# A fused attention and mixture-of-experts kernel: a list turned three units later, first weights loaded in four separate steps, one more side step in a slot

## The chip, the cores and the metric

The kernel runs on one core of one Trainium2 chip. The metric is the device time in microseconds (us) of one execution; lower is better. The core's engines are TensorE (PE, with its weight loads shown as PEld), VectorE (DVE), ScalarE (ACT), GpSimd (POOL) and SyncE (SP). In this kernel SP issues nearly all direct transfers, and POOL issues the indirect ones (gathers and scatters through a list of rows).

## The reference

Eight batches of attention with 12 heads, 448 tokens and head size 64, with a sigmoid in place of the softmax, followed by a mixture of experts over all 3584 tokens (768 wide, 8 experts, 1024 hidden units). All data is float32.

```python
scores = scale * np.matmul(q, k.transpose(0, 1, 3, 2)) - np.log(S)
attn = 1.0 / (1.0 + np.exp(-scores))
x = np.matmul(attn, v)            # then (batch*seq, heads*head_dim) = (3584, 768)

logits = x @ w_gate
e_idx = np.argmax(logits, axis=1)
gate_w = softmax(logits)[np.arange(N), e_idx]
eom = 1.0 / (1.0 + np.exp(-(x @ w_output_gate)))
for e in range(E):
    mask = e_idx == e
    h = np.maximum(x[mask] @ w1[e], 0.0)
    out[mask] = gate_w[mask, None] * eom[mask, e, None] * (h @ w2[e])
```

## The kernel before, in words

**Attention.** `attention` runs 168 units, one after the other. The text counts them backwards from the end of attention, as the code does (`self.unit(u - U * NG)`): unit -168 is the first, unit -1 the last. Seven units make a group, which holds two pairs of heads. In unit u, PE computes scores of u (L632), ACT applies the sigmoid (L634), and PE multiplies the result of unit u-2 with the values (L641). The scores have two places in PSUM, so the scores of u+2 need the sigmoid of u to be done. Where a pair of heads is complete, DVE adds its two halves out of PSUM and turns the sum (`evict`: L644 or L648, L654, L655). After every second group, PE multiplies four such results with the gate weights (`gates`, L671); these read the tiles that L654 writes. One such place is unit -11.

**Work beside attention.** `unit(u)` is called at the head of each unit and puts extra work into the engines' queues at that place: the first tokens are sorted to experts before attention ends. At unit -28 the first expert's layer-1 weights start to load (`load_w`, L416, issued by SP), and from unit -22 on they are split into a high and a low part (L426 on ACT, L427 on DVE). At unit -18 the first list of tokens is turned (`spread_lists`: a DVE transpose at L388, then twelve small POOL copies at L392 to L395), POOL gathers the rows of the first slot (L404), and SP loads two more lists from DRAM (`load_list`, L383). At unit -13 these two are turned by a second `spread_lists`; at unit -10 the whole layer-2 weights of the first expert are loaded in four pieces of 768 KB (`load_w2`); at unit -8 the gathered rows are turned (`turn_x`, L452).

**Slots.** Then come slots of 256 tokens of one expert each. Slot 0, 1 and 2 are made from the first six batches. `slot` runs layer 1 for eight blocks of hidden units f (`layer1_mm`, L467 and L468; ACT copies one PSUM half at L475, DVE adds the other at L476 into `gl`), and the PSUM places of layer 1 are three, so block f+3 waits for L476 of block f. Then come four outputs of layer 2 (L490 to L492; ACT scales them at L502, POOL scatters them at L504 after the second and the fourth). Beside it the next slot's rows are gathered, turned (L452) and split (L427), and its weights are split (`split_w1`: ACT L430, DVE L433; `split_w2`: ACT L426, DVE L427). An order "high, low" in layer 1 means that PE needs the low part of weight pair k (L433) at steps d = 2k and 2k+1 of block 0.

**Side work.** The generator `side` in `build` holds the rest of the routing: the last batch's gates, the table of all remaining slots (`table(True)`, DVE lines L299 to L368 in five pieces, each on one partition), and the loading and turning of the remaining lists. `slot` takes one step of it (`next(side, None)`) after each of the blocks f = 0 to 6, once more in slot 0, and after the second, third and fourth layer-2 output.

**Order.** Nothing reorders the instructions: `manual_schedule` keeps each engine's queue in the order in which the code emits it. An engine that waits holds up all that stands behind it in its queue.

Of the kernel before, what the change touches and what calls it, by code (L numbers as in the profile page):

```python
# [51 lines left out]
class Kernel:  # L52
# [455 lines left out]
    def slot(self, cur, nxt, side=None, begun=False, drain=False):  # L508
        nx = self.load_slot(*nxt) if nxt is not None else None
        if drain:  # L510
            self.gather(dict(lx=self.lxb[:, 1], xg=self.half_x(1)))
            self.nc.gpsimd.drain()
        self.split_w2(0)
        for f in range(8):
            self.layer1(f, begun and f == 0)
            if f:
                self.high_low(f - 1)
            if f in (1, 3, 5):
                self.split_w2(f // 2 + 1)
            if side is not None and f < 7:  # L520
                next(side, None)
        self.high_low(7)
        if side is not None and begun:
            next(side, None)
        self.load_w2(nx)
        if nx is not None:
            self.high_w1(0)
            self.turn_x(nx)
            for k in range(3):
                self.split_x(nx, k)  # L530
            self.low_w1(0)
        for i, (t, n) in enumerate(((0, 0), (0, 1), (1, 0), (1, 1))):
            self.layer2(cur, t, n, self.ys[t])
            if i < 2 and nx is not None:
                self.split_w1(i + 1)
            if side is not None and i > 0:
                next(side, None)
        return nx

# [177 lines left out]
    def unit(self, u):  # L717
        if u == -161:
            self.row_words()
        if u == -154:  # L720
            self.init_list()
        if u == -31:
            self.tgen = self.table(False)
        if -31 <= u < -28:
            next(self.tgen)
        if u == -28:
            self.s0 = self.slot_regs(self.tab_e, 0, self.lts[:, 0], self.lxs[:, 0])
        s = self.s0 if u >= -28 else None
        for d in range(6):
            if u == -28 + d:  # L730
                self.load_w(s, self.w1, self.w1r, [d], 1)
            if u == -22 + 2 * d:
                self.split_w1_row(d)
        if u == -21:
            self.load_list(self.tab_e, 0, self.lr_e[0][0:8], 8)
        if u == -18:
            self.spread_lists(self.lr_e[0], self.lts[:, 0:1], self.lxs[:, 0:1])
            self.gather(s, ROWS_E)
            for k in range(1, EARLY):
                self.load_list(self.tab_e, k, self.lr_e[1][8 * k - 8:8 * k], 8)  # L740
        if u == -13:
            self.spread_lists(self.lr_e[1], self.lts[:, 1:EARLY], self.lxs[:, 1:EARLY])
        if u == -10:
            self.load_w2(s)
        if u == -8:
            self.turn_x(s)
        for k, at in enumerate((-6, -5, -4)):
            if u == at:
                self.split_x(s, k)
# [120 lines left out]
```

## Time and profile before

| | us |
|---|---|
| median of three runs (lowest, highest) | 802.03 (799.63, 804.19) |
| the profiled execution's own time | 802.2 |
| its span, first to last instruction | 800.4 |
| PE busy in the span | 784.6 (98%) |
| DVE busy | 498.4 (62%) |
| ACT busy | 494.9 (62%) |
| POOL busy | 338.4 (42%) |

The durations below come from that one profiled execution, and times of day are microseconds from its span's start. Attention ends and slot 0 begins at about 285; slot 0 ends at about 320, slot 1 at 356, slot 2 at 390. A busy PE is not PE at its peak, so time that PE loses shows in two ways: as idle time, and as work that takes longer than the same work elsewhere. "Granted clock" (PEclk) is the share of TensorE's full clock that the chip gave in a stretch.

### The profile page before, as it was taken

The numbers are of one execution on the slowest core, as the hardware profiler recorded it, in microseconds if no ns is written. First come the engines' busy times: TensorE is split into PE (matmuls) and PEld (weight loads), VectorE is DVE, ScalarE is ACT, GpSimd is POOL, SyncE is SP. The second block draws the span as 40 slices with busy tenths as digits, with TensorE's granted clock in tenths as the row PEclk, the third lists the DMA queues.
The fourth block names the chain that finished last, engine by engine and source line by source line (L and its number), as shares of the span: only waits on it lengthen the run. The fifth ranks groups of instructions, "written<-read, shape, count | busy, mean of one in ns | idle before, by whom it ended". The sixth has DMA issues, their size and how long they took to land. (4 is left out here: it accounts for less than half of the span.)

```text
span 800.4 us, 15091 instructions
## 1 busy us (share of the span) xinstructions
PE 784.6 (98%) x5772; PEld 582.3 (73%) x5772; DVE 498.4 (62%) x731; ACT 494.9 (62%) x665; POOL 338.4 (42%) x454
## 2 busy tenths in 40 slices
PE   9999999999999899899999999999999999999996
PEld 4333433333333379799999999999999999999885
DVE  2344435444455667877785657766667767667687
ACT  5666666666668556556665556655666557565685
POOL 4003302310333456647646265543646725445344
PEclk9999999999999999999999999999999999999999
DMA  6353553525448420237228471182274211749382
GB/s 255 131 209 128 158 200 139 193 85 208 170 173 347 154 90 21 77 123 266 75 75 290 166 270 51 49 312 79 61 259 156 64 45 41 267 131 336 110 314 59
DMA packets 32311, 126.80 MB, mean 158 GB/s; under 512 B 5536, under 2 KB 7824, under 8 KB 28257
## 3 DMA queue, kind: packets, MB, share of 16 engines
q1 hardware_dynamic: 22288, 100.81, 35.5%
q0 software_dynamic: 9936, 24.88, 9.4%
q8 instruction: 50, 0.82, 0.4%
q14 instruction: 37, 0.29, 0.1%
HBM read 153.15 MB, written 23.64 MB: 221 GB/s over the span
## 5 line engine op out<-in xcount | busy, mean ns | idle before, releaser
L467 PE MATMUL ps<-rounded 128*128 128x512 f32 x672 | 234.8, 393 | 2.0 <-DVE gl L476 2.0
L634 ACT ACTIVATE a<-ps,bias_s 128x896 f32<-128x896 f32 x168 | 169.2, 1008 | 102.5 <-PE ps L632 96.1
L468 PE MATMUL ps<-rounded 128*128 128x256 f32 x672 | 188.1, 280 | 0.0
L404 POOL DMA_INDIRECT plain<-x_dram,lxs x120 | 170.2, 1418 | 38.3 <-issue 37.0
L490 PE MATMUL ps<-w2h,h 128*128 128x384 f32 x480 | 160.6, 335 | 0.0
L492 PE MATMUL ps<-w2h,h 128*128 128x384 f32 x480 | 160.4, 334 | 0.0
L491 PE MATMUL ps<-w2l,h 128*128 128x384 f32 x480 | 160.4, 334 | 0.0
L632 PE MATMUL ps<-kqv 64*64 64x448 f32 x1344 | 158.6, 543 | 0.5 <-ACT a L634 0.4
L641 PE MATMUL ps<-a,kqv 64*64 64x448 f32 x1344 | 156.7, 538 | 0.0
L427 DVE TENSOR_TENSOR w2l<-plain,w2h 128x1536 fp32r<-128x1536 f32 x60 | 105.3, 1758 | 78.3 <-ACT w2h L426 68.1
L467 PEld LDWEIGHTS ps<-rounded 128*128 128x128 f32 x672 | 125.7, 187 | 31.3 <-DVE gl L476 2.7
L504 POOL DMA_INDIRECT out<-y,lts x28 | 59.7, 2132 | 172.3 <-ACT y L502 92.5
L468 PEld LDWEIGHTS ps<-rounded 128*128 128x128 f32 x672 | 127.0, 189 | 0.0
L641 PEld LDWEIGHTS ps<-a,kqv 64*64 64x64 f32 x1344 | 51.7, 134 | 75.5 <-issue 74.8
L632 PEld LDWEIGHTS ps<-kqv 64*64 64x64 f32 x1344 | 48.8, 133 | 75.1 <-issue 62.3
L433 DVE TENSOR_TENSOR rounded<-plain,rounded 128x2048 fp32r<-128x2048 f32 x46 | 102.8, 2284 | 0.0
L426 ACT CAST w2h<-plain 128x1536 fp32r<-128x1536 f32 x60 | 88.2, 1473 | 5.4 <-PE ps L671 4.4
L490 PEld LDWEIGHTS ps<-w2h,h 128*128 128x128 f32 x480 | 90.1, 188 | 0.7
L491 PEld LDWEIGHTS ps<-w2l,h 128*128 128x128 f32 x480 | 90.1, 188 | 0.1
L492 PEld LDWEIGHTS ps<-w2h,h 128*128 128x128 f32 x480 | 90.1, 188 | 0.0
L475 ACT COPY gl<-ps 128x256 f32<-128x256 f32 x112 | 41.7, 372 | 77.7 <-PE ps L468 73.3
L430 ACT CAST rounded<-plain 128x2048 fp32r<-128x2048 f32 x46 | 87.6, 1904 | 0.0
(186 smaller groups left out, 649.0 us busy)
## 6 DMA issues: line engine op xcount, KB each, us to landing
plain<-w SPq DMA_DIRECT2D x68, 768.0 KB
plain<-w SPq DMA_DIRECT2D x48, 1024.0 KB
kqv<-kqv SPq DMA_DIRECT2D x23, 1344.0 KB
x_dram<-xt SPq DMA_DIRECT2D x8, 1344.0 KB
plain<-w SPq DMA_DIRECT2D x6, 512.0 KB
plain<-x_dram,lxs POOLq DMA_INDIRECT x120
kqv<-kqv SPq DMA_DIRECT2D x1, 896.0 KB
lst<-plain POOLq DMA_DIRECT2D x1, 726.0 KB
```

The lines of the kernel that those rows point to most:

```text
L404: self.nc.gpsimd.indirect_dma_start(out=s["xg"][:, g], out_offset=None, in_=x4, in_offset=bass.IndirectOffsetOnAxis(ap=s["lx"][:, g:g + 1] ...
L426: self.nc.scalar.copy(hi, raw)
L427: self.nc.vector.tensor_tensor(lo, raw, r32(hi), ALU.subtract)
L433: self.nc.vector.tensor_tensor(self.w1p[1][k], self.w1r[:, 2 * k:2 * k + 2], r32(self.w1p[0][k]), ALU.subtract)
L467: nc.tensor.matmul(ps, wh[d][:, c], self.xc[:, d].rearrange("p a t -> p (a t)"), start=(d == 0), stop=False)
L468: nc.tensor.matmul(ps[:, 0:TS], wl[d][:, c], self.xc[:, d, 0], start=False, stop=(d == 5))
L490: nc.tensor.matmul(ps, hh[:, f, tk], wh, start=(f == 0), stop=False)
L491: nc.tensor.matmul(ps, hh[:, f, tk], wl, start=False, stop=False)
L492: nc.tensor.matmul(ps, hl[:, f, tk], wh, start=False, stop=(f == 7))
L632: nc.tensor.matmul(ps[half[h], j, 0:S], kg[half[j], e, 0, o:o + 64], kg[half[j], e, 1], start=True, stop=True)
L634: nc.scalar.activation(at[u % 4], ps[:, :, 0:S], AF.Sigmoid, bias=self.bias_s, scale=1.0 / math.sqrt(D))
L641: nc.tensor.matmul(self.ps_o[e][h][half[j], 0:S], v[half[h], 6 if i == 3 else 3 * e + c, j], a[half[h], j], start=(i in ((0, 3 if h else 4 ...
```

## The change

Three edits. In `unit`, the second `spread_lists` (two lists at once) moves from unit -13 to unit -10. The load of the layer-2 weights, four pieces at unit -10, becomes four loads of one piece each at units -9, -7, -5 and -3, each behind a DVE memset of one element of the place that it writes, so that SP's load waits for DVE to get there. In `slot`, a step of the side work is taken behind the first layer-2 output too, so each slot with side work takes one step more, and every later step comes earlier by one, then by two, and so on.

```diff
@@ -533,7 +533,7 @@
             self.layer2(cur, t, n, self.ys[t])
             if i < 2 and nx is not None:
                 self.split_w1(i + 1)
-            if side is not None and i > 0:
+            if side is not None:
                 next(side, None)
         return nx
 
@@ -738,10 +738,12 @@
             self.gather(s, ROWS_E)
             for k in range(1, EARLY):
                 self.load_list(self.tab_e, k, self.lr_e[1][8 * k - 8:8 * k], 8)
-        if u == -13:
+        if u == -10:
             self.spread_lists(self.lr_e[1], self.lts[:, 1:EARLY], self.lxs[:, 1:EARLY])
-        if u == -10:
-            self.load_w2(s)
+        for k in range(4):
+            if u == -9 + 2 * k:
+                self.nc.vector.memset(self.w2r[0:1, 2 * k, 0:1], 0.0)
+                self.load_w(s, self.w2, self.w2r, [2 * k])
         if u == -8:
             self.turn_x(s)
```

In DVE's queue near the end of attention, the turn of the two lists (L388) stood at unit -13, ahead of the eviction (L648, L654) whose tile the gates of unit -11 read (`lt_99` is the turned list, `xh` and `x_161` the evicted sums):

```order
 L655 STREAM_TRANSPOSE xt_164<-x_160 128x14x32
 L427 TENSOR_TENSOR rounded<-plain,rounded 128x1024
-L388 STREAM_TRANSPOSE lt_99<-plain 32x192
 L648 COPY xh<-ps 128x448
 L654 TENSOR_TENSOR x_161<-xh,ps 128x448
```

Now that eviction follows L427 directly. A few rows on, behind the two copies of the gates' results (L683, L678), the turn comes back, and the first of the memsets (L745, into `plain`, where the layer-2 weights land) one unit behind it:

```order
 L683 TENSOR_TENSOR gl_113<-gl_113,ps 64x448
 L678 COPY gl_114<-ps 64x448
-L644 COPY xh<-ps 128x448
+L388 STREAM_TRANSPOSE lt_99<-plain 32x192
+L644 COPY xh<-ps 128x448
+L745 MEMSET plain 1x1
 L654 TENSOR_TENSOR x_158<-xh,ps 128x448
 L655 STREAM_TRANSPOSE xt_164<-x_158 128x14x32
```

In DVE's queue at the border of slot 0 and slot 1, the pieces of the table (L299 to L356) move forward past the split of the third weight pair (the last L433) and past the split (L427) and the sum (L476) with which slot 1 begins:

```order
 L427 TENSOR_TENSOR rounded<-plain,rounded 128x2x256 x3
-L433 TENSOR_TENSOR rounded<-plain,rounded 128x2048 x3
+L433 TENSOR_TENSOR rounded<-plain,rounded 128x2048 x2
 L299 COPY hb<-last_e 1x1
```

```order
 L353 TENSOR_SCALAR hb<-slots,hb 1x15
 L356 SCALAR_TENSOR_TENSOR hb<-hb 1x15 x3
-L476 TENSOR_TENSOR gl_113<-gl_113,ps 128x256
-L481 SCALAR_TENSOR_TENSOR h_2445<-gl_113,h_2444 128x256
-L427 TENSOR_TENSOR w2l_2447<-plain,w2h 128x1536
+L427 TENSOR_TENSOR w2l_2451<-plain,w2h 128x1536
+L476 TENSOR_TENSOR gl_113<-gl_113,ps 128x256
 L358 TENSOR_SCALAR hb<-hb 1x15
```

So the first piece of the table now stands ahead of the third L433, and the fourth ahead of slot 1's first L427 and L476 (the numbers behind `w2l` and `h` differ only in counting). The later steps move too: in POOL's queue the twelve copies of one more list stand ahead of slot 1's first scatter, and those of the next list ahead of slot 2's gather instead of behind it.

## Rows read from the trace of the kernel before

**Rows 1.** The page: busy time of each engine with its share of the span.

```profile
PE 784.6 (98%) x5772; PEld 582.3 (73%) x5772; DVE 498.4 (62%) x731; ACT 494.9 (62%) x665; POOL 338.4 (42%) x454
```

**Rows 2.** The waits of PE over the whole span, longest in total first: who waited for whom, us in total, times, longest.

```profile
PE ps L671 <- DVE x L654: 2.1, 1, 2.1
PE ps L467 <- DVE gl L476: 2.0, 2, 1.5
```

**Rows 3.** DVE in order of time, units -14 to -11: start, duration, what, and in brackets the idle time before it and what ended it.

```profile
255.51 1.24 DVE L427 TENSOR_TENSOR rounded<-plain,rounded 128x1024 fp32r<-128x1024 f32 x1 [0.57 <-ACT rounded L426]
260.96 0.50 DVE L388 STREAM_TRANSPOSE lt<-plain 32x192 f32<-32x192 f32 x1 [4.21 <-DMA plain<-lst]
...
262.00 0.62 DVE L654 TENSOR_TENSOR x<-xh,ps 128x448 f32<-128x448 f32 x1
```

**Rows 4.** PE in order of time: the scores of units -13 and -11, the gates of unit -11 with a wait ahead of them, the scores of unit -10, and those of unit -1.

```profile
255.49 0.93 PE L632 MATMUL ps<-kqv 64*64 64x448 f32 x8
...
258.81 0.98 PE L632 MATMUL ps<-kqv 64*64 64x448 f32 x8
...
262.68 0.95 PE L671 MATMUL ps<-x,wg 128*32 128x448 f32 x6 [2.13 <-DVE x L654]
...
265.64 1.77 PE L632 MATMUL ps<-kqv 64*64 64x448 f32 x8
...
281.67 0.93 PE L632 MATMUL ps<-kqv 64*64 64x448 f32 x8
```

**Rows 5.** ACT in order of time: the sigmoids of units -55 and -43 (six groups earlier, the same places of their groups as units -13 and -1), those of units -13 and -12, and the first split of the layer-2 weights in slot 0.

```profile
187.88 1.01 ACT L634 ACTIVATE a<-ps,bias_s 128x896 f32<-128x896 f32 x1 [0.50 <-PE ps L632]
...
208.16 1.01 ACT L634 ACTIVATE a<-ps,bias_s 128x896 f32<-128x896 f32 x1 [0.49 <-PE ps L632]
...
257.75 1.01 ACT L634 ACTIVATE a<-ps,bias_s 128x896 f32<-128x896 f32 x1 [1.36 <-PE ps L641]
...
264.17 1.01 ACT L634 ACTIVATE a<-ps,bias_s 128x896 f32<-128x896 f32 x1 [4.48 <-remote]
...
288.13 1.48 ACT L426 CAST w2h<-plain 128x1536 fp32r<-128x1536 f32 x1 [4.40 <-PE ps L671]
```

**Rows 6.** Busy time in three stretches: length, then busy us of PE, PEld, DVE, ACT and POOL, the granted clock, the busy share of the DMA engines and GB/s; and, from SP in order of time, the four loads of the layer-2 weights (first issue, time until the last is issued).

```profile
240.00:248.00 8.00, 8.00 (x92) 3.24 (x88) 4.62 (x6) 7.18 (x8) 0.00 (x0) 1.00 1.01 411
252.00:260.00 8.00, 7.86 (x86) 3.08 (x80) 3.64 (x4) 6.18 (x7) 6.54 (x13) 1.00 1.00 362
...
266.00:267.00 1.00, 1.00 (x8) 0.25 (x4) 0.99 (x2) 0.76 (x1) 0.40 (x3) 0.50 1.00 398
...
255.47 8.56 SPq L416 DMA_DIRECT2D plain<-w  x4
```

**Rows 7.** DVE in order of time, end of slot 0 and beginning of slot 1: the three L433 (merged), the first and last row of the table's first piece, slot 1's first L427, the sum of block 0, the first row of the table's fourth piece, the sum of block 1, the first row of the fifth piece, the sum of block 2.

```profile
313.96 6.69 DVE L433 TENSOR_TENSOR rounded<-plain,rounded 128x2048 fp32r<-128x2048 f32 x3
320.57 0.14 DVE L299 COPY hb<-last_e 1x1 f32<-1x1 f32 x1
...
322.77 0.15 DVE L317 SCALAR_TENSOR_TENSOR hb<-hb,ebase 1x8 f32<-1x8 f32 x1
...
326.14 1.74 DVE L427 TENSOR_TENSOR w2l<-plain,w2h 128x1536 fp32r<-128x1536 f32 x1
327.81 0.40 DVE L476 TENSOR_TENSOR gl<-gl,ps 128x256 f32<-128x256 f32 x1
328.14 0.26 DVE L348 TENSOR_TENSOR hb<-hb 1x120 f32<-1x120 f32 x1
...
329.47 0.40 DVE L476 TENSOR_TENSOR gl<-gl,ps 128x256 f32<-128x256 f32 x1
...
331.81 0.15 DVE L358 TENSOR_SCALAR hb<-hb 1x15 f32<-1x15 f32 x1
...
332.86 0.40 DVE L476 TENSOR_TENSOR gl<-gl,ps 128x256 f32<-128x256 f32 x1
```

**Rows 8.** PE in order of time, slot 1: the first matmul of block 0, of block 3 and of block 5.

```profile
320.38 0.39 PE L467 MATMUL ps<-rounded 128*128 128x512 f32 x1
...
328.27 0.50 PE L467 MATMUL ps<-rounded 128*128 128x512 f32 x1 [1.49 <-DVE gl L476]
...
333.31 0.50 PE L467 MATMUL ps<-rounded 128*128 128x512 f32 x1 [0.54 <-DVE gl L476]
```

**Rows 9.** POOL in order of time: the first scatter of slot 1, the first of the twelve copies of a turned list, the second scatter, the first and the last of the eight gathers of slot 2; then DVE's turn of the gathered rows and the three L433 of slot 2 (merged), and PE's first matmul of slot 3 that reads the third weight pair's low part.

```profile
350.11 3.15 POOL L504 DMA_INDIRECT out<-y,lts  x1 [5.76 <-ACT y L502]
...
355.06 0.20 POOL L392 CAST lxs<-wg 32x32 int32<-32x32 f32 x1 [1.80 <-DVE wg L388]
...
359.74 1.41 POOL L504 DMA_INDIRECT out<-y,lts  x1 [2.65 <-ACT gl L475]
361.45 0.99 POOL L404 DMA_INDIRECT plain<-x_dram,lxs  x1 [0.30 <-issue]
...
371.31 0.94 POOL L404 DMA_INDIRECT plain<-x_dram,lxs  x1 [0.30 <-issue]
...
376.84 1.78 DVE L452 STREAM_TRANSPOSE plain<-plain 128x1536 f32<-128x1536 f32 x1 [0.19 <-issue]
...
381.12 6.69 DVE L433 TENSOR_TENSOR rounded<-plain,rounded 128x2048 fp32r<-128x2048 f32 x3
...
391.21 0.28 PE L468 MATMUL ps<-rounded 128*128 128x256 f32 x1
```

## The prediction, made before the changed kernel ran

> **What bounds the kernel now.** I read the page first: PE is busy 98% of the span and no other engine above 62% [rows 1], so time can only come from PE's gaps and from PE work that runs slower than elsewhere. The list of PE's waits is short: 2.1 us once, for DVE's L654, and 2.0 us in two places, for DVE's L476 [rows 2]. The changed lines touch both. Then I read DVE, PE and ACT in order of time around each wait.
>
> The first wait is at unit -11. DVE finished L427 of unit -14 at 256.75 and stood 4.21 us before the turn of the second list (L388), whose data landed only at 260.96. L654, whose tile the gates read, was queued behind it and ended at 262.62 [rows 3]. PE, idle since 260.55, began the gates at 262.68 [rows 4]. That is not all of the price. The reader should compare equal stretches: from unit -13 to unit -1 PE's scores took 281.67 - 255.49 = 26.18 us [rows 4]; the same places of their groups, units -55 to -43, took 208.16 - 187.88 = 20.28 us by ACT's sigmoids, which follow the scores directly there [rows 5]. So 5.9 us are lost in these twelve units, and 2.1 of them are the wait that the list names.
>
> The rest shows in three rows. Behind the wait the granted clock stood at 0.50 [rows 6], the lower of its two levels (1.2 GHz), and the scores of unit -10 took 1.77 us in place of 0.93 [rows 4]. ACT's sigmoid of unit -13 came 1.3 us behind the end of its scores, which held the scores of unit -11 back by 0.3 us (the next-but-one scores need its PSUM place). And ACT's sigmoid of unit -12 began only at 264.17, after 4.48 us of idle that the profile puts down to "remote", while its scores had been done since about 258 [rows 4, 5]; the scores of unit -10, which need its place, started at 265.64, right behind it. So two things held PE back here one after the other: the gates, then ACT. ACT's lateness falls in a stretch in which the DMA engines were fully busy and POOL gathered at the same time; between 240 and 248 they were as busy (1.01, 411 GB/s) without a gather, and PE kept its clock and was never idle [rows 6].
>
> **The list and the weights.** The list's transfer was issued ahead of the layer-2 weights, so its landing at 260.96 is at worst the same. The turn now stands behind L678 of unit -11: without the wait the gates run from about 260.5 to 261.5, the two copies behind them (0.62 each, as L654) end near 262.7, so the turn finds its list there with 1.7 us to spare. What is late next would be ACT: I think that its 4.48 us go too, since the weights, which SP issued from 255.47 to 264.03 beside the gather [rows 6], now begin at unit -9, with the gather nearly over. I keep 0.3 us of loss for the lateness at unit -13, which came when only one piece of the weights had been issued. Gain: 5.9 - 0.3 = 5.6 us. Its bounds are 0 (ACT stays late until 264.17 whatever DVE does) and 5.9.
>
> The four memsets write one element; the nearest row is a copy of one element, 0.14 us [rows 7], so four make 0.6 us of DVE, beside an attention in which DVE has 3.6 to 4.6 of 8 us busy [rows 6]: nothing. SP's loads now wait for DVE: behind each stand only the next piece and the write of the last batch's rows, which waits for the end of attention anyway. The last piece leaves at unit -3, some 4.5 us before the end of attention; a piece of 768 KB takes 2 us at the 398 to 411 GB/s of the full stretches [rows 6]; the first use is ACT's L426 at 288.13, behind attention's end [rows 5], that of the last piece five blocks of layer 1 later. If that cover were gone, ACT and DVE in slot 0 would wait, but it is over 10 us.
>
> **The side step.** In slot 0 the order on DVE decides. From 313.96 to 329.87 DVE has no pause: three L433, the table's first three pieces, L427, L476 of block 0, the fourth piece, L476 of block 1 [rows 7]. PE meets it twice: block 3 waits 1.49 us for L476 of block 0, block 5 0.54 us for that of block 2 [rows 8]. Now the first piece (320.57 to 322.92, 2.35 us) stands ahead of the third L433, which ends at 323.0 in place of 320.65. Block 0 of slot 1 starts at 320.38 and a block takes 2.1 us, so its fifth step needs that low part at 322.0: a new wait of 1.0 us. The fourth piece (328.14 to 329.47, 1.33 us) stands ahead of L476 of block 0, which ends at 329.54 in place of 328.21: block 3 starts at 329.6 in place of 328.27. The new wait lies inside that: it only splits it. Two blocks later block 5 could start at 333.8; L476 of block 2 has the same DVE work ahead of it as before and is done at 333.3, so the wait of 0.54 goes. Against 333.31 PE is 0.5 us later. Cost: 0.5 us. The bounds: 0 if block 0 loses nothing, 1.33 if the wait at block 5 stays.
>
> In slots 1 and 2 POOL's order changes. The twelve copies of one list (0.20 each, 2.4 us in all) stand ahead of slot 1's first scatter, and those of the next ahead of slot 2's gather [rows 9]. The first twelve began at 355.06 behind DVE's turn; that turn now stands one L433 (2.2 us) earlier, so they take from 352.8 to 355.2, and the scatter that began at 350.11 begins then. With 1.4 us for itself and the 6.5 us that the second scatter began behind its end before (359.74 - 353.26), then 1.7 us for the second and 2.4 for the copies, the gather starts at 367.2 in place of 361.45, 5.8 us later; with less lag between the scatters it is 2 us. The gather ends its issue at 372.25 and L452 follows at 376.84 without waiting for it; with an estimated 2 us to land there are 2.6 us to spare, and the third L433 of that slot ends at 387.81, 3.4 us before PE needs it at 391.21 [rows 9]. So 6 us of lateness are covered, and I cost it at 0, with 2 us as the upper end.
>
> By the Trainium skill, page "SBUF — State Buffer", section "SBUF: two separate sides", POOL can't write descriptors while DVE holds the port that they share. The scatter that took 3.15 us beside L433 against 1.41 us without one agrees [rows 9]; by that rule a gather that slides further into slot 2 meets more of DVE's long rows, which is the third rival below.
>
> **The sum.** 802.2 (the profiled execution) - 5.6 + 0.5 = 797.1. The three runs shown have their median 0.2 lower, so I say 797.0.
>
> **Rivals.** First, the list wasn't the last to come. If ACT's signal is late for a reason that the change doesn't touch, the scores of unit -10 still wait for 265.2, PE idles and loses its clock as before, and only the 0.5 of the side step is left: 802.5. For it: ACT's late start ended behind L654, not before, and the profile can't name its cause. Against it: nothing like it shows between 240 and 248 at the same DMA load [rows 6].
>
> Second, the longer wait in slot 1 costs the clock. The waits at blocks 0 and 3 are 1.0 and 2.0 us in place of one of 1.49. Behind the gates' 2.1 us and the thin work after it a stretch of some 3.2 us ran at 0.50, which loses 1.6 us: 798.7. Against it: in the 1.49 us of before nothing fell.
>
> Third, slower: slot 2's gather. If it starts 5.8 us late and each of its eight issues takes twice the 1.41 us that the first seven took on average (371.31 - 361.45), as the scatter beside L433 took twice, it ends at 367.2 + 8 x 2.8 = 389.6, and L452 runs at 391.6, 14.8 us later than before. From 3.4 us on every us is PE's: 11.4 us lost, 797.1 + 11.4 = 808.5. The kernel turns slower than before where L452 slips by more than 8.5 us, to 385.4 or later. For it: gather, lists and the next weights fall together there. Against it: DVE's work in layer 1 is the same as before, and the gather ran beside it at 1.41.
>
> **How the numbers follow.** Chances: the forecast 0.61 (own range 795.5 to 799), no gain at unit -11 0.18, the clock lost in slot 1 0.12, the late gather 0.09, of which nearly all ends above 802. What can be told from no change is 0.5%, here 4 us: faster means below 798.0. The forecast lies below it in about four of five cases of its own range (0.49), the clock rival in one of four (0.03): faster 0.52. Slower, above 806, only the gather at its worst and an unlucky mix: 0.07. Same: 0.41. The range from 794.8 to 802.7 takes in the first rival and leaves out the gather and a gain beyond the 5.9.
>
> **What would show it.** Right: no PE wait for L654; L388 at unit -10 without idle time before it; units -13 to -1 in 20.3 to 20.8 us at a granted clock of 1.00; the four loads apart by two units each; a wait of PE at block 0 of slot 1 for L433 and one of about 2 us at block 3, none at block 5. Wrong: ACT's sigmoids still several us behind their scores near unit -12; a granted clock below 1.00 around block 3 of slot 1; PE waits at the beginning of slot 3 for L433, with L452 of slot 2 waiting for its gather. The forecast as a whole fails if the twelve units keep more than 2 us of their loss.

## The result: 0.8% slower, and the profile after

| | median, us | lowest to highest | runs |
|---|---|---|---|
| before | 800.08 | 798.37 to 804.19 | 18 |
| changed | 806.61 | 802.47 to 809.05 | 18 |

The ratio is 1.0076, with a 95% interval of 1.0064 to 1.0089. The forecast was 797.0, the range 794.8 to 802.7: the sign was wrong. The profiled execution of the changed kernel took 806.6 us, its span 804.9.

The page of the changed kernel, busy time of each engine; beside [rows 1] POOL has 4 us more and PE 2 us:

```profile
PE 786.6 (98%) x5772; PEld 584.8 (73%) x5772; DVE 498.6 (62%) x735; ACT 494.0 (61%) x665; POOL 342.6 (43%) x454
```

The waits of PE over the changed kernel's whole span, as in [rows 2] (who waited for whom, us in total, times, longest):

```profile
PE ps L490 <- ACT y L502: 4.8, 2, 4.1
PE ps L468 <- DVE rounded L433: 3.1, 1, 3.1
PE ps L695 <- DVE rounded L691: 1.3, 1, 1.3
PE ps L574 <- DVEq L825: 1.2, 1, 1.2
PE ps L467 <- DVE gl L476: 0.5, 1, 0.5
```

The wait for L654 is gone. Two new ones stand at the top: for L502, which was in no wait of before, and for L433. To see what they cost, cut the span at the first matmul of each slot. From slot 2 on, a slot in which PE never waits takes 33.28 us; slots 0 and 1 are compared with the kernel before:

| kernel | units -13 to -1 | slot 0 starts | slot 0 | slot 1 | slot 2 | slot 3 to the end |
|---|---|---|---|---|---|---|
| before, as profiled first | 26.18 | 284.78 | 35.60 | 35.94 | 33.28 | 410.8 |
| before, a second profile | 23.00 | 281.79 | 35.62 | 36.10 | 33.28 | 410.7 |
| changed | 20.95 | 280.35 | 36.50 | 38.89 | 39.20 | 410.0 |

Against the second profile of before (an experiment, below) the change gains 1.4 us up to slot 0 and 0.75 behind slot 2, and loses 0.9, 2.8 and 5.9 us in the three slots: 7.4 in all, which is 804.9 - 797.5.

**Units.** In order of time, PE's scores of units -13 and -1 in the changed kernel, and DVE's turn of the list, now at unit -10:

```profile
256.29 0.93 PE L632 MATMUL ps<-kqv 64*64 64x448 f32 x8
...
277.24 0.93 PE L632 MATMUL ps<-kqv 64*64 64x448 f32 x8
...
263.22 0.52 DVE L388 STREAM_TRANSPOSE lt<-plain 32x192 f32<-32x192 f32 x1
```

The turn waits for nothing, and the twelve units take 277.24 - 256.29 = 20.95 us.

**Slots 0 and 1.** POOL in order of time, the changed kernel: the four scatters of the last-but-one batch's rows to the lists (L280), and the first gather of slot 0 behind them.

```profile
278.04 0.99 POOL L280 DMA_INDIRECT lst<-meta,posi  x1 [0.67 <-POOL meta L278]
282.53 0.93 POOL L280 DMA_INDIRECT lst<-meta,posi  x1 [3.50 <-DMA lst<-meta,posi]
287.60 0.93 POOL L280 DMA_INDIRECT lst<-meta,posi  x1 [4.14 <-DMA lst<-meta,posi]
289.93 1.82 POOL L280 DMA_INDIRECT lst<-meta,posi  x1 [1.40 <-DMA lst<-meta,posi]
...
292.18 0.99 POOL L404 DMA_INDIRECT plain<-x_dram,lxs  x1 [0.16 <-issue]
```

The same in the second profile of before:

```profile
279.68 0.99 POOL L280 DMA_INDIRECT lst<-meta,posi  x1 [0.67 <-POOL meta L278]
282.06 0.93 POOL L280 DMA_INDIRECT lst<-meta,posi  x1 [1.40 <-DMA lst<-meta,posi]
285.51 0.93 POOL L280 DMA_INDIRECT lst<-meta,posi  x1 [2.51 <-DMA lst<-meta,posi]
289.00 0.93 POOL L280 DMA_INDIRECT lst<-meta,posi  x1 [2.56 <-DMA lst<-meta,posi]
...
290.33 0.99 POOL L404 DMA_INDIRECT plain<-x_dram,lxs  x1 [0.16 <-issue]
```

Each scatter waits until the one before it has landed. Slot 0 starts 1.4 us earlier in the changed kernel, yet its gather starts 1.9 us later: 11.8 us behind the slot's start in place of 8.5. All that POOL does for the routing stands behind that gather, and in DVE's queue L452 stands behind L276, which waits 5.7 us for POOL's L272. At the border of slots 0 and 1, DVE and PE of the changed kernel in order of time (L299 begins the table's first piece):

```profile
308.55 1.78 DVE L452 STREAM_TRANSPOSE plain<-plain 128x1536 f32<-128x1536 f32 x1 [0.20 <-issue]
...
312.83 4.49 DVE L433 TENSOR_TENSOR rounded<-plain,rounded 128x2048 fp32r<-128x2048 f32 x2
317.23 0.13 DVE L299 COPY hb<-last_e 1x1 f32<-1x1 f32 x1
...
319.40 2.29 DVE L433 TENSOR_TENSOR rounded<-plain,rounded 128x2048 fp32r<-128x2048 f32 x1
...
321.75 0.58 PE L468 MATMUL ps<-rounded 128*128 128x256 f32 x1 [3.12 <-DVE rounded L433]
...
328.39 0.50 PE L467 MATMUL ps<-rounded 128*128 128x512 f32 x1 [0.45 <-DVE gl L476]
```

L452 comes 28.2 us behind the start of slot 0, in both profiles of before at 24.9; in the first of them the three L433 began 29.2 us behind the start [rows 7], now they begin at 32.5.

**Slot 2.** The changed kernel in order of time: POOL's first copy of the twelve, one of the later ones, the two scatters of slot 1, a copy of the next twelve, the first and the last gather of slot 2; DVE's turn of the list and the two rows beside which the slow copies ran; then L452 and what follows it on ACT and PE.

```profile
354.75 2.18 POOL L392 CAST lxs<-wg 32x32 int32<-32x32 f32 x1 [9.28 <-DVE wg L388]
...
358.04 1.71 POOL L395 COPY lts<-wg 32x8 f32<-32x8 f32 x1
...
360.43 1.03 POOL L504 DMA_INDIRECT out<-y,lts  x1 [0.16 <-issue]
366.54 2.45 POOL L504 DMA_INDIRECT out<-y,lts  x1 [5.08 <-ACT w2h L426]
...
372.99 1.00 POOL L404 DMA_INDIRECT plain<-x_dram,lxs  x1 [0.15 <-POOL lts L395]
...
382.10 0.94 POOL L404 DMA_INDIRECT plain<-x_dram,lxs  x1 [0.30 <-issue]
...
354.17 0.51 DVE L388 STREAM_TRANSPOSE wg<-hb 32x192 f32<-32x192 f32 x1
354.62 2.24 DVE L433 TENSOR_TENSOR rounded<-plain,rounded 128x2048 fp32r<-128x2048 f32 x1
...
357.92 1.79 DVE L427 TENSOR_TENSOR w2l<-plain,w2h 128x1536 fp32r<-128x1536 f32 x1 [0.60 <-ACT w2h L426]
...
385.10 1.78 DVE L452 STREAM_TRANSPOSE plain<-plain 128x1536 f32<-128x1536 f32 x1 [9.83 <-DMA plain<-x_dram,lxs]
...
386.91 1.66 ACT L426 CAST rounded<-plain 128x512 fp32r<-128x512 f32 x3 [10.30 <-DVE plain L452]
388.47 0.57 ACT L502 ACTIVATE y<-ps,lts 128x384 f32<-128x384 f32 x1
...
389.10 0.44 PE L490 MATMUL ps<-w2h,h 128*128 128x384 f32 x1 [4.08 <-ACT y L502]
```

Read it as a chain. POOL stands 9.28 us before the first copy, for a turn that DVE reaches only behind two L433; in before the first scatter was issued meanwhile, at 350.11 [rows 9]. The second scatter starts 6.1 us behind the first (the profile names ACT's L426 as what ended its wait, which gives it nothing; but the trace has the first scatter landing 5.3 us behind the start of its issue, at 365.7, and the second begins 0.8 us after that). Then twelve more copies, then the gather. On ACT the three splits of the turned rows (L426) stand ahead of L502, which empties the first output's PSUM place: PE waits 4.08 us for it. And the wait takes the clock with it. Windows of the changed kernel behind it (columns as in [rows 6]):

```profile
388.00:390.00 2.00, 0.90 (x4) 0.91 (x5) 2.00 (x4) 2.00 (x4) 0.00 (x0) 0.86 0.00 0
390.00:392.00 2.00, 2.00 (x8) 2.00 (x7) 2.00 (x2) 2.00 (x3) 0.41 (x1) 0.50 0.00 0
392.00:394.00 2.00, 2.00 (x11) 2.00 (x10) 2.00 (x2) 1.58 (x2) 2.00 (x1) 0.79 0.00 0
394.00:396.00 2.00, 2.00 (x14) 1.88 (x13) 2.00 (x1) 0.86 (x2) 0.75 (x1) 1.00 0.37 147
```

PE is busy from 390 on, yet its records count 8 matmuls in 390 to 392 and 14 in 394 to 396, at the full clock: the lower level (1.2 GHz) adds 1.8 us to the wait, 5.9 in all.

### The profile page after: what moved, and what is told of

It is laid out like the page before. It is cut to its first block, busy times and chain, and to the rows that moved or that the text cites. A ratio compares the mean times of both kernels' runs of the same rounds, so it can differ in the third digit from the quotient of the medians.

```text
span 804.9 us, 15094 instructions
## 1 busy us (share of the span) xinstructions
PE 786.6 (98%) x5772; PEld 584.8 (73%) x5772; DVE 498.6 (62%) x735; ACT 494.0 (61%) x665; POOL 342.6 (43%) x454
## 5 line engine op out<-in xcount | busy, mean ns | idle before, releaser
L404 POOL DMA_INDIRECT plain<-x_dram,lxs x120 | 168.6, 1405 | 38.1 <-issue 36.3
L427 DVE TENSOR_TENSOR w2l<-plain,w2h 128x1536 fp32r<-128x1536 f32 x60 | 105.4, 1759 | 66.1 <-ACT w2h L426 66.0
L433 DVE TENSOR_TENSOR rounded<-plain,rounded 128x2048 fp32r<-128x2048 f32 x46 | 102.9, 2283 | 0.1
L426 ACT CAST w2h<-plain 128x1536 fp32r<-128x1536 f32 x60 | 88.2, 1473 | 5.5 <-PE ps L671 4.4
```

The source lines that it names most:

```text
L404: self.nc.gpsimd.indirect_dma_start(out=s["xg"][:, g], out_offset=None, in_=x4, in_offset=bass.IndirectOffsetOnAxis(ap=s["lx"][:, g:g + 1] ...
L426: self.nc.scalar.copy(hi, raw)
L427: self.nc.vector.tensor_tensor(lo, raw, r32(hi), ALU.subtract)
L433: self.nc.vector.tensor_tensor(self.w1p[1][k], self.w1r[:, 2 * k:2 * k + 2], r32(self.w1p[0][k]), ALU.subtract)
```

## The experiments

The theory after the first reading: two separate losses, both a gather that POOL reaches late. The four loads delay the scatters ahead of slot 0's gather; the side step puts copies ahead of slot 1's scatter and slot 2's gather. Rivals: one of the edits does all the damage. The table gives all runs, cut as above (us from each profile; the ratio to before, measured beside it, with its interval). The kernel before itself took 799.2 to 799.8 us as a median in the runs of the experiments, but 804.89 beside the three marked with a star.

| kernel | units -13 to -1 | slot 0 starts | slot 0 | slot 1 | slot 2 | slot 3 to the end | ratio |
|---|---|---|---|---|---|---|---|
| units only | 21.26 | 279.82 | 36.46 | 39.00 | 33.32 | 412.8 | 1.0055 (1.0034 to 1.0076) |
| side step only | 22.82 | 281.69 | 35.61 | 36.31 | 39.21 | 410.0 | 1.0047 (1.0031 to 1.0063) |
| list only | 23.00 | 281.78 | 35.61 | 36.05 | 33.28 | 410.9 | 1.0008 (0.9992 to 1.0025) |
| pieces only | 20.98 | 279.49 | 36.49 | 39.06 | 33.52 | 412.8 | 1.0038 (1.0019 to 1.0057) |
| loads at -9 to -6 | 21.04 | 280.01 | 35.64 | 36.04 | 33.28 | 413.8 | 0.9984 (0.9967 to 1.0001) |
| loads at -7 to -4 * | 24.96 | 283.75 | 35.49 | 36.28 | 34.17 | 413.1 | 0.9990 (0.9970 to 1.0009) |
| changed, loads at -9 to -6 * | 26.07 | 284.91 | 35.61 | 36.51 | 39.13 | 410.9 | 1.0025 (1.0007 to 1.0042) |
| scatter ahead again | 22.06 | 281.35 | 35.65 | 36.50 | 35.10 | 411.3 | 1.0026 (1.0012 to 1.0041) |
| gather ahead again, 1st | 23.28 | 282.37 | 35.50 | 36.68 | 42.20 | 410.0 | 1.0109 (1.0086 to 1.0132) |
| gather ahead again, 2nd * | 25.39 | 284.29 | 35.50 | 36.45 | 40.48 | 410.0 | 1.0064 (1.0043 to 1.0085) |
| gather ahead again, 3rd | 22.06 | 280.66 | 35.62 | 36.53 | 36.89 | 412.9 | 1.0063 (1.0042 to 1.0083) |

**The edits apart.** Units only: the changed kernel with the side step's line as before.

```diff
-            if side is not None:
+            if side is not None and i > 0:
```

> The two edits in the units, with the side step as before. Theory (two late gathers): the units give their 5.2 us, but the four loads of weights now run beside the scatters of the last-but-one batch (L280), so POOL reaches slot 0's gather some 3.2 us later behind the slot's start (11.8 in place of 8.6 us). L452 of slot 0 follows 3.3 us later, the third L433 ends about 39.2 us behind the start of slot 0, where PE needs it at 38.3: waits of about 1 us for L433 and 0.7 us for L502, and none in slot 2. Time 797.5. Rival 1 (the unit edits do all the damage, the side step none): slot 2's gather is late too, PE waits about 4 us for L502 at its second output, 805 to 806. Rival 2 (the side step does all of it): no wait at the border of slots 0 and 1 beyond those of before, 795.2.

Measured: 803.97 (9 runs), 0.55% slower. The gather of slot 0 starts 11.8 us behind the slot's start (279.82 to 291.64), as the theory had it. PE's waits in this kernel:

```profile
PE ps L467 <- DVE gl L476: 2.7, 1, 2.7
PE ps L468 <- DVE rounded L433: 2.5, 3, 1.0
...
PE ps L490 <- ACT y L502: 0.6, 1, 0.6
```

Slot 1 loses as much as in the changed kernel (39.00 against 38.89), only at another place: with the table's pieces behind the third L433, the wait for L433 is 1.0 us and that for L476 2.7. Slot 2 loses nothing. So both rivals fall, and the theory's time of 797.5 too: it took the gain in the units for 5.2 us, the whole difference between the changed kernel and the first profile of before. From slot 3 on this kernel loses 2.1 us more than the second profile of before (412.8 against 410.7), which the theory did not have: PE waits 0.96 us for L433 in slot 3 and 0.53 in slot 5.

The first scatter of the last-but-one batch starts at 277.50 here and is waited for 3.79 us; in the kernel with the list's move only, below, it starts at 279.66 and is waited for 1.40. Windows over the two waits (columns as in [rows 6]; the last but one is the DMA engines' busy share), units only and then list only:

```profile
278.00:280.00 2.00, 2.00 (x22) 0.63 (x14) 0.28 (x2) 0.77 (x1) 0.49 (x1) 1.00 0.86 272
...
280.00:282.00 2.00, 2.00 (x21) 0.67 (x14) 0.28 (x2) 0.73 (x1) 0.65 (x1) 1.00 0.08 10
```

Side step only: before with that line of the change alone.

> The side step behind the first output alone, the units as before. Theory (two late gathers): at the border of slots 0 and 1 a wait of about 1 us for the third L433; in slot 1 the twelve copies ahead of the first scatter, and twelve more ahead of slot 2's gather, put that gather about 10 us later, L452 waits for it, and PE waits 2 to 4 us for L502 in slot 2 and loses its clock behind it. Time 803.5 (802 to 806). Rival 1 (the side step costs nothing unless the unit edits made slot 1 late): 800.6, no wait in slot 2. Rival 2: as the theory, and above 806.

Measured: 803.14 (12 runs), 0.47% slower, as the theory had it. Slot 2 takes 39.21 us, as in the changed kernel, with the units as before; slot 1 only 0.2 more than in the second profile of before. In order of time, the scatters and the first gather on POOL, then L452:

```profile
358.30 1.03 POOL L504 DMA_INDIRECT out<-y,lts  x1 [0.16 <-issue]
363.70 1.00 POOL L504 DMA_INDIRECT out<-y,lts  x1 [4.38 <-ACT h L480]
...
368.46 2.56 POOL L404 DMA_INDIRECT plain<-x_dram,lxs  x1 [0.15 <-POOL lts L395]
...
381.81 1.78 DVE L452 STREAM_TRANSPOSE plain<-plain 128x1536 f32<-128x1536 f32 x1 [9.36 <-DMA plain<-x_dram,lxs]
```

List only and pieces only: before with one half of the edits in the units.

```diff
-        if u == -13:
+        if u == -10:
             self.spread_lists(self.lr_e[1], self.lts[:, 1:EARLY], self.lxs[:, 1:EARLY])
```

> Only the turn of the second list moved from unit -13 to unit -10; the four weight loads stay in one burst at unit -10, the side step as before. All theories: PE's wait for L654 goes, and POOL's scatters of the last-but-one batch run as before (gather 8.6 us behind the start of slot 0). If ACT's late signal hangs on the burst of weights beside the gather, ACT's sigmoid of unit -12 stays several us late and the units -13 to -1 keep 2 to 4 us of their 5.9: 797 to 799. If it was only the list: the units take about 20.6 us, 794.7.

> Only the weight loads in four steps at units -9 to -3; the turn of the second list stays at unit -13, the side step as before. Theory (two late gathers): PE's wait for L654 of about 2 us stays or shrinks, ACT's late signal goes, so the units win 2 to 4 us; POOL's scatters of the last-but-one batch are about 3 us late again, which costs 1.5 us at the border of slots 0 and 1: 797.5 to 800. If the weights have no part in POOL's lateness, the gather of slot 0 starts 8.6 us behind the slot's start: 796 to 798.

Measured: 799.45 (no difference) and 803.31 (0.38% slower). The list's move wins nothing: the wait for L654 goes, but PE then waits 1.6 us in unit -5 for ACT's L262, which stands behind a split of slot 0's rows until these have landed and DVE has turned them; units -13 to -1 take 23.00 us, as in the second profile of before. The pieces alone bring the 2 us: DVE's turn of slot 0's rows comes at 267.80 without waiting for the gather, in the second profile of before at 270.63 after 2.79 us of waiting, and PE's wait for L262 is gone. They alone also bring the loss in slots 0 and 1. Both guesses for the list missed, and of the two for the pieces the times missed while the late gather came (11.8 us).

**Was the 5.9 us there?** The kernel before, unchanged, with a second profile.

> The kernel before, unchanged, for a second profile. Theory (the 5.9 us belonged to that one execution): units -13 to -1 take about 22.8 us, as they did in the run with the side step alone, whose units are the same; the wait for L654 is about 0.6 us in place of 2.1, slot 0 starts near 281.7 in place of 284.8, and the execution takes 799. Rival (the loss is regular and the side step or its run were the exception): 26 us, slot 0 at 284.8, 802.

Measured: 799.3; units -13 to -1 take 23.00 us, the wait for L654 is 0.56, slot 0 starts at 281.79. Three of the 5.9 us were not there.

**Where the loads may lie.** The two unit edits, the four loads packed.

```diff
-            if u == -9 + 2 * k:
+            if u == -9 + k:
```

> The two edits in the units, side step as before, but the four weight loads at units -9, -8, -7, -6 in place of -9, -7, -5, -3. Theory (the last loads delay the scatters of the last-but-one batch, and these the gather of slot 0): the first scatter lands without the extra 2.4 us, the gather of slot 0 starts 8.5 to 9.5 us behind the slot's start in place of 11.8, slot 1 takes 36 in place of 39.0 us, slot 0 35.6 in place of 36.5; of the 2 us won in the units some may go to a later turn of the gathered rows. Time 797.5 to 799.5. Rival (the scatters are late for the write of the last batch's rows and the next weights, which the loads don't change): slot 1 stays at 39 us, 803.5.

Measured: 798.35 against 799.81, a ratio of 0.9984 whose interval just reaches 1. POOL in this kernel:

```profile
277.90 0.99 POOL L280 DMA_INDIRECT lst<-meta,posi  x1 [0.67 <-POOL meta L278]
280.29 0.93 POOL L280 DMA_INDIRECT lst<-meta,posi  x1 [1.39 <-DMA lst<-meta,posi]
...
288.55 0.99 POOL L404 DMA_INDIRECT plain<-x_dram,lxs  x1 [0.16 <-issue]
```

The first scatter lands in 1.39 us of waiting, the gather starts 8.5 us behind the slot's start, and slots 0 and 1 are as before: the loads were the cause. Of the 2 us won, slots 3, 5 and 6 lose about 1 each in the profile (34.4, 34.1 and 34.3 us; the second profile of before has one such slot). In each of them PE waits for L433 at the beginning (0.88, 0.49 and 0.45 us), as L452 of the slot before came late (24.91 us behind the start of slot 2; 20.5 and 22.7 in the two profiles of before).

With `u == -7 + k` the last load leaves one unit earlier than in the change.

> The two edits in the units, side step as before, the four loads at units -7, -6, -5, -4. Theory (the loads should lie between the landing of slot 0's gather and the first scatter of the last-but-one batch): the turn L452 no longer waits its 1.5 us for the gather, units -13 to -1 take 20.6 in place of 21.0 us, and the first scatter waits 1.4 us or a little more; slot 1 36 to 37 us, 797.5 to 799. Rival (the last load, one unit before that of the kernel with the loads two units apart, still delays the first scatter): slot 0's gather 10 us or more behind the slot's start, slot 1 38 us or more, 801.

Measured: no difference (0.9990). The first scatter waits 2.98 us, between 1.39 (last load at -6) and 3.79 (at -3, units only); the gather is back at 8.6 us, and slot 1 takes 36.3. The units ran with a stall of another kind, below, so nothing can be said of the 20.6.

**Are the two losses separate?** The changed kernel with the packed loads.

> The changed kernel with its four weight loads at units -9, -8, -7, -6: all three edits, the loads packed. Theory (two separate losses, one from the loads beside the scatters, one from the side step): slot 0 takes 35.6 and slot 1 36.3 us as with the side step alone, slot 2 keeps 39.2 us; 3.5 us less than the changed kernel, some 803. Rival (the losses aren't separate: without the late scatters the copies no longer hurt): slot 2 33.3 us, 797 to 798.

Measured: slots 0, 1 and 2 at 35.61, 36.51 and 39.13, as the theory had them one by one; 0.25% slower than before, where the changed kernel is 0.76% slower. They are separate.

**Inside the side step's loss.** Four kernels have the side step alone and shift single turns of lists by changing the number of pauses ahead of each. First the twelve copies back behind slot 1's first scatter, the next twelve still ahead of the gather:

```diff
-                for _ in range(3):
+                for _ in range((3, 4, 2, 3)[min(i, 3)]):
```

> The side step alone, with the turns of the lists shifted so that the twelve copies of one list stand behind slot 1's first scatter again, while the next twelve stay ahead of slot 2's gather. Theory (what delays that gather is above all the first scatter held behind the copies, and the second behind the first): the gather starts about 8 us behind the start of slot 2 in place of 14.9, L452 near 21.5 in place of 28.2, slot 2 takes 33.3 in place of 39.2; 0.3 us slower than before, about 799.5. Rival (the copies ahead of the gather cost most): slot 2 still 37 to 39 us, 802 to 803.

Measured: 0.26% slower, slot 2 35.10 in place of 39.21. The gather starts at 13.5 us, not 8: the copies ahead of it took 4.3 us, and the second scatter came at 6.9 in place of 3.5. The copies ahead of the scatter are most of slot 2's loss, but not all; and slot 3 takes 1.25 us longer in exchange, with a wait of 0.97 for L433, so that from slot 2 on 2.8 of the 5.2 us come back.

For the reverse, `(3, 3, 4, 2)`: copies ahead of the scatter, the gather ahead of the next twelve.

> The side step alone, with the turns shifted so that the twelve copies stay ahead of slot 1's first scatter, while the next twelve stand behind slot 2's gather again. Theory: both scatters are as late as with the side step alone, the gather starts about 11.3 us behind the start of slot 2 in place of 14.9, L452 near 25, just at the 25.3 us behind the start from which PE waits: slot 2 33.3 to 34.5 us, about 800. Rival (the copies ahead of the gather cost nothing, the first scatter all): slot 2 37 to 39 us, 802 to 803.

> As the earlier try with slot 2's gather ahead of its twelve copies again, but the turn of the list after it one step later, so that DVE doesn't wait in slot 2 for a list that was loaded two steps before. The twelve copies ahead of slot 1's first scatter stay. Theory (both lots of copies delay the gather, each some 4 us): the gather starts about 10.5 us behind the start of slot 2 in place of 14.9 with the side step alone, its L452 comes 4 us earlier, near 24 us, slot 2 takes 33.3 to 34.5 us and the kernel about 800.5. Rival (the held first scatter does it all): slot 2 stays at 37 to 39 us, 802.5 to 804.

> As the two earlier tries with slot 2's gather ahead of its twelve copies, now with the turn of the last list a slot later, so that DVE waits in slot 2 neither for that list nor for POOL's copies; the twelve copies ahead of slot 1's first scatter stay. Theory (the place in the slot at which the gather starts decides, since from about 14 us on it shares the DMA engines with the weights of the next slot, and PE waits if L452 comes later than about 25.3 us behind the slot's start): the gather starts near 10.5 us, L452 comes at 24 to 26 us, slot 2 takes 33.3 to 35.5 us, the kernel 0.3% slower to equal. Rival (a gather that starts behind about 9 us lands with the last of those weights, wherever it starts): L452 near 28 us as with the side step alone, slot 2 38 to 39 us, 0.5% slower.

The first try made a wait of its own: DVE stood 9.77 us before the turn of a list that had not landed, and PE behind it. The second, `(3, 3, 4, 3)`, made another: DVE stood 7.28 us before a turn whose place POOL's copies still had to read. Both say nothing of the question. The third, with `(3, 3, 4, 3, 9)[i]`, is clean in slot 2: the gather starts 10.1 us behind the slot's start, 4.7 earlier than with the side step alone, but L452 comes only 1.1 us earlier, at 27.1, and slot 2 takes 36.89. It lies between the theory's 24 to 26 and the rival's 28: a gather that is still going then shares the DMA engines with the next slot's layer-2 weights (SP issues four loads of 768 KB from 16.5 us on in this kernel, and the engines' share is 1.02 from 20 to 24 us) and lands when they are nearly through. From slot 3 on this kernel takes 2.9 us more than with the side step alone; 1.3 of them are a longer wait behind the last full slot (L574, 2.5 in place of 1.2 us), and the rest stays open, so its ratio is no measure of slot 2.

These kernels show for slot 2 what the prediction lacked:

| kernel | L452 behind the slot's start | PE's wait for L502 | slot 2 above 33.28 |
|---|---|---|---|
| before, first and second profile | 20.5, 22.7 | none | 0, 0 |
| loads at -7 to -4 | 25.88 | 0.60 | 0.9 |
| scatter ahead again | 26.82 | 1.54 | 1.8 |
| gather ahead again, 3rd | 27.06 | 1.77 | 3.6 |
| changed, loads at -9 to -6 | 28.12 | 2.84 | 5.9 |
| side step only | 28.20 | 2.92 | 5.9 |
| changed | 29.36 | 4.08 | 5.9 |

In each row with a wait it is L452's place less 25.28 us. From 1.77 us on the slot loses far more than the wait; there the granted clock behind the wait fell to 0.50, while behind 1.54 us it stayed at 1.00. Another slack is smaller and shows only in the next slot: where PE was not held for L502, it waited for L433 at the beginning of the next slot for L452's place less some 24.0 us (24.53 gave 0.50 in the second profile of before, 24.91 gave 0.88 with the loads at -9 to -6).

## Why the prediction was wrong, step by step

**The list and the weights, gain 5.6.** The signs came as forecast (20.95 us, clock 1.00, no wait for L654, no idle ahead of L388), but the term was mis-sized: the 5.9 us were measured against equal units of the same execution, and taken to be lost in every execution. The second profile loses 23.00 - 20.28 = 2.7. What the edits win is 1.7 to 2.1 us (20.95 to 21.26 against 23.00), and by the two halves run apart all of it is the loads', none the list's: the wait for L654 hid another one, for ACT's L262, which the prediction did not have. The other 3 us came with ACT's "remote" wait [rows 5], and the first rival was right that this doesn't hang on the list. It shows again in the three starred kernels, in two of them with the list at unit -10 and none of the four loads under way. ACT and PE of the changed kernel with packed loads:

```profile
265.96 1.90 ACT L634 ACTIVATE a<-ps,bias_s 128x896 f32<-128x896 f32 x2 [5.21 <-remote]
...
259.87 0.98 PE L632 MATMUL ps<-kqv 64*64 64x448 f32 x8 [0.96 <-issue]
```

Its loads begin only at 269.50, and the share of the DMA engines was 0.28 from 262 to 266. So what the prediction held responsible, the weights beside the gather, falls too, and the cause stays open.

**The loads, cost nothing.** This step failed. The prediction named what stands behind the loads in SP's queue and their first use, but not who shares the DMA engines with them: the four scatters of the last-but-one batch, each waiting for the one before, ahead of a gather, ahead of the chain that ends in L433. The engines' share beside the first of them was 0.86 with the loads apart and 0.08 with the burst (units only, list only). Price: 0.9 us in slot 0 and 2.8 to 2.9 in slot 1, more than the 2 us won.

**The side step, cost 0.5 at the border of slots 0 and 1.** Right in its waits, and the cost was smaller: 0.2 to 0.3 us in slot 1 (36.31 against 36.10 and 36.05), with a wait for L433 of 0.7, one at block 3 of 1.7 and none at block 5 (side step only). In the changed kernel the late L452 came on top, hence 3.1.

**The side step in slots 1 and 2, cost 0.** This step failed worst: 5.9 us. The order was read rightly, the times behind it not. The first twelve copies were to begin at 352.8 on before's clock, 3.5 us ahead of slot 2; they began 1.0 us ahead of it, since slot 1's own gather and L452 were late. Part of that came with the side step itself: two scatters ahead of that gather, now beside the moved L433 and L427, ran 2.97 and 2.23 us in place of 0.93 and 0.99. The twelve copies took 5.5 us in place of 2.4: the first ran 2.18 us and ended with the L433 beside it, another 1.71 beside L427, where the rest take 0.2. By the Trainium skill, page "SBUF — State Buffer", section "SBUF: two separate sides", the port pair that DVE and POOL share is an exclusive lock, held for a whole instruction. These rows agree, and the prediction had applied it to scatters and gathers only, not to copies. So the first scatter came 4.7 us behind slot 2's start where -1.1 was forecast, and the gather at 17.3 where 10.9 was. The 2 us that were estimated for its landing held here (its issue ended at 383.04, L452 began at 385.10), but not where the next slot's weights were still under way: 5.3 us in the second profile of before, 5.7 in the third try with the gather ahead.

**The third rival** had the place and the sign, and 808.5 against 806.6 measured, but not the mechanism, so the near hit is luck. It let the eight issues take 2.8 us each beside DVE's long rows; they took 1.30 (372.99 to 382.10 for seven), with DVE idle beside six of them, and the lateness came before the gather, from copies and scatters. L452 slipped by 8.8 us behind its slot's start, past the 8.5 that the rival named; it had 0.09. The slack that was counted to L433 in slot 3, 3.4 us, was right (20.5 + 3.4 = 23.9 us, 24.0 in the runs), but with L452 at 29.4 PE was held one step earlier, for L502 behind ACT's L426, a chain that the prediction did not follow.

**The clock rival** named waits of 1.0 and 2.0 us in slot 1. With the side step alone these came as 0.7 and 1.7, and the clock stayed at 1.00. It fell in the changed kernel, but behind waits of 3.1 and 4.1 us that the rival did not have.

## What to carry to other kernels

A stall in one profiled execution is not yet a gain: compare its time with the spread of the runs, and look for it in a second profile before pricing its removal. For every transfer and every small instruction that is moved, list what shares its DMA engines and what stands behind it in its queue, down to the next chain that ends at the critical engine; scatters that wait for one another add up what each loses. Measure the slack to every wait that hangs on a transfer, not to one: here L452 has two, some 24.0 us behind its slot's start for the wait for L433 in the next slot (where nothing held PE before), and 25.28 for the dearer one for L502 in the same slot.

## What the runs showed that was not expected

Between 257 and 267 four profiles of fourteen (the first of before, and the three starred ones) have ACT idle for 3.2 to 5.3 us in front of a sigmoid with no releaser ("remote"), and PE stops beside it that the profile puts down to "issue"; the other ten have none. In the changed kernel with packed loads the DMA share was 0.28 from 262 to 266, so full DMA engines aren't needed for it. It didn't follow the edits: the same kernel before has it in one profile and not in the other. The three starred kernels ran together on one chip, and no other kept profile is known to come from that chip; whether the chip is the reason isn't shown.

The clock can cost as much as the wait: a wait of 1.77 us cost slot 2 3.6 and one of 2.92 us 5.9, while 1.54 us cost 1.8; and a wait of 4.08 us cost no more than one of 2.92. Behind the 2.92 us the granted clock stood at 0.50 for some 5.5 us of PE's work, behind the 4.08 us for some 3.3.
